# Loading K and Q two rows to a partition, and turning them head by head

## The chip, the cores and the metric

The kernel runs on one core of a Trainium2 chip. A core has TensorE (PE: matmuls, with weight loads shown apart as PEld), VectorE (DVE), ScalarE (ACT), GpSimd (POOL) and SyncE (SP), which here mostly issues transfers, and 16 DMA engines that carry out what SP, ACT and POOL issue. Matmul results lie in PSUM, all other tiles in SBUF. The metric is the time of one execution on the device in microseconds; less is better.

## The reference

Block-sparse attention, followed by a mixture of experts that sends each token to one expert. Cut to what matters:

```python
# q, k, v: (4, 8, 768, 64) float32; blocks of 32 rows, 24 blocks
scores = scale * np.matmul(q, k.transpose(0, 1, 3, 2))
mask = np.abs(blk_i - blk_j) <= 1
mask = mask | (blk_i == 0) | (blk_j == 0) | (blk_i == 23) | (blk_j == 23)
for qb in range(24):
    for kb in sampled_blocks[qb]:          # three random blocks for each
        mask[qb*32:(qb+1)*32, kb*32:(kb+1)*32] = True
attn = softmax(np.where(mask, scores, -1e9))
x = (attn @ v).transpose(0, 2, 1, 3).reshape(3072, 512)
# router: cosine of x with 8 expert vectors, softmax, one expert per token
logits = normalized(x) @ normalized(expert_emb).T / tau
e, gate = argmax(logits), softmax(logits).max()
out[token] = gate * (relu(x[token] @ w1[e]) @ w2[e])   # w1: 8x512x1024
```

## The kernel before, in words

The attention comes first (`attention_fast`), then the experts (`expert_tiles`), whose weights of some 4 MB a tile are loaded by SP while TensorE works on the tile before. A second, exact form of the attention is in the program for data that the fast form cannot take; it has its own loads (`load_pair`) and is not run here. The diff does not touch it.

**Tiles of the attention.** A batch has 768 rows, cut in six chunks of 128 (the chunks are shifted by one block, so that a chunk's first rows meet the first and the last block; chunk 0 is made of rows 736 to 767 and 0 to 95, and `pieces` gives the two row ranges). Two batches are worked on together: pair `s` of 12 stands for one chunk in two batches, and `n` = 2s + i is one chunk of one batch. There are 24 such units, and the main loop runs one in each step; the order is `TURNS` = 0, 2, 1, 3, 4, 5 and so on.

**One step.** For the unit `now`, `score_near` multiplies K with the turned Q (`qt`): neighbouring blocks (L550) and the first and last block (L553); `score_far` does the same with the gathered random blocks `kg` (L575). ScalarE takes exponentials (L558, L560, L580). For the unit of the step before, `weigh_near` and `weigh_far` multiply the exponentials with V (L630), and `normalize` divides and writes `x`. For the unit before that, `turn_x` turns x (L707) and copies it out (L709), and `part_logits` and `sum_logits` make the router's logits (L727, L736). Between the two halves of `weigh_far`, `turn_q` turns the Q of the next unit. Chunk 0 and the last pair of steps have in addition `score_ends` and `weigh_ends`, since the first and the last block see all keys.

**Turning.** Scores need the head dimension on the partitions, so rows of K and Q are turned on TensorE with an identity matrix as the moving operand.
- `load_k` fetches a head pair of one batch: `kraw` has row `p` of chunk `c` on partition `p`, and beside each other the 64 elements of the two heads. `turn_k` turns each chunk's 128 x 128 square (L501: six for a head pair) into two PSUM banks, and one copy (L503) of 128 x 768 brings it to `kt`, on ScalarE for odd head pairs and on VectorE for even ones. After a batch's last pair ScalarE copies the two edge blocks to the end of `kt` (L506).
- `load_q` fetches a pair `s`: a row on each partition, with both batches and eight heads of 64 elements. `turn_q` turns four squares of two heads each (L514) into the one PSUM bank that `turn_x` uses too (`xg_ps`), and two VectorE copies of 64 x 512 (L519) bring them to `qt`, the first head of each couple to partitions 0 to 63 and the second to 64 to 127. The rest of `qt` stays zero, which keeps the heads apart.

**Order.** The attention is written out by hand: each engine works its instructions in the order in which the program gives them (`manual_schedule`). K of the first batches (head pairs 0 to 7) is turned ahead of the loop and in steps 0 and 1; pairs 8 to 15 are turned in steps 10, 11 and 12 (two, three and three pairs), and there the K gathers of `gather_k` (L532, L536, shared between VectorE and GpSimd) come after the turning. The PSUM tiles `ac`, `dps`, `bps` and `kps` take turns on two buffers (`big`).

**Transfers.** SP issues nearly all of them in program order, through `fetch_all`: the V gathers of the pair to come (L478, `vg`, 12 of 128 KB, in one of two buffers, so that they wait until `weigh_far` has freed it), and between each two of these one other load (L476; L480 when no gathers are left): Q, K, or V itself (`vt`). `route` writes x to memory (L834). The first Q loads alone are issued by ScalarE. K has six buffers of a head pair, Q two of a pair.

Of the kernel before, what the change touches and what calls it, by code (L numbers as in the profile page):

```python
# [12 lines left out]
F32 = mybir.dt.float32  # L13
# [7 lines left out]
P = 128  # L21
B, H, S, D = 4, 8, 768, 64
# [3 lines left out]
NC = S // P  # L26
NPAIR = H // 2
# [3 lines left out]
ND, NF = DM // P, F // P  # L31
# [22 lines left out]
DUO = 2  # L54
# [264 lines left out]
def pieces(c, shifted=True):  # L319

    if not shifted:
        return [(slice(0, P), c * P)]
    if c:
        return [(slice(0, P), c * P - BLK)]
    return [(slice(0, BLK), S - BLK), (slice(BLK, P), 0)]
# [61 lines left out]
def pair_chunk(s):  # L387

    a, at = divmod(s, NC)
    return a, at if a == 0 else (at + 1) % NC  # L390
# [8 lines left out]
def of_seq(src, a, i=None):  # L399

    if i is None:
        return src[DUO * a:DUO * (a + 1)].rearrange("i h s d -> s (i h) d")
    return src[DUO * a + i].rearrange("h s d -> s h d")


def in_pair(t, i=None):

    return t.rearrange("p i h e -> p (i h) e") if i is None else t[:, i]


def load_q(k, s, i=None):

    a, c = pair_chunk(s)
    if ("q", s) not in k.raw:
        k.raw["q", s] = k.ld.tile([P, DUO, H, D], F32, name="qraw", tag="qraw", bufs=2)
    t, src = in_pair(k.raw["q", s], i), of_seq(k.q, a, i)
    return [(t[rows], src[lo:lo + rows.stop - rows.start]) for rows, lo in pieces(c)]


def load_k(k, g):  # L420

    b, j = divmod(g, NPAIR)
    k.raw["k", g] = t = k.kld.tile([P, NC, 2, D], F32, name="kraw", tag="kraw", bufs=6)
    return [(t[:, :, h], k.k[b, 2 * j + h].rearrange("(c p) d -> p c d", p=P)) for h in range(2)]


def load_v(k, a, m, i=None):
# [65 lines left out]
def turn_k(k, g):  # L493

    nc = k.nc
    b, j = divmod(g, NPAIR)
    kt = k.kt[b % 2]
    raw = k.raw.pop(("k", g))
    ps = k.big.tile([P, 2, 512], F32, name="kps", tag="big")
    for c in range(NC):  # L500
        nc.tensor.transpose(ps[:, c // 3, c % 3 * P:(c % 3 + 1) * P], raw[:, c].rearrange("p h d -> p (h d)"), k.ident)  # L501
    copy = nc.scalar.copy if g % 2 else nc.vector.tensor_copy
    copy(out=kt[:, j, 0:S].rearrange("p (w t) -> p w t", w=2), in_=ps[:, :, 0:3 * P])  # L503
    if j == NPAIR - 1:
        for i, block in enumerate((NB - 1, 0)):
            nc.scalar.copy(out=kt[:, :, S + i * BLK:S + (i + 1) * BLK], in_=kt[:, :, block * BLK:(block + 1) * BLK])  # L506


def turn_q(k, n):

    raw = in_pair(k.raw["q", n // DUO], n % DUO)
    ps = ring(k, "xg_ps", 0, 1, k.eps, [P, ND, P])
    for j in range(NPAIR):
        k.nc.tensor.transpose(ps[:, j], raw[:, 2 * j:2 * j + 2, :].rearrange("p h d -> p (h d)"), k.ident)  # L514
    k.qt[n] = t = k.qt_ring[k.queries % 2]
    k.queries += 1
    for h in range(2):
        rows = slice(D * h, D * (h + 1))
        k.nc.vector.tensor_copy(out=t[rows, :, h], in_=ps[rows])  # L519


def gather_k(k, n):
# [543 lines left out]
def ring(k, name, i, n, pool, shape):  # L1066

    key = name, i % n
    if key not in k.rings:
        k.rings[key] = pool.tile(shape, F32, name=f"{name}_{i % n}")  # L1070
    return k.rings[key]
# [191 lines left out]
def attention_fast(n, ctx):  # L1263
# [44 lines left out]
    for m in range(2, NC):  # L1308
        fetch_all(n, (), load_v(n, 0, m, 0))
    turn_q(n, 0)  # L1310
    for g in range(NPAIR):
        turn_k(n, g)
        if g + 6 < 2 * NPAIR:
            fetch_all(n, (), load_k(n, g + 6))
# [21 lines left out]
    for s in range(NCH + 1):  # L1336
# [49 lines left out]
        for g in turning.get(s, ()):  # L1386
            turn_k(n, g)
# [282 lines left out]
```

## Time and profile before

| what | value |
|---|---|
| time of the runs shown | 634.98 us median of 3 (632.53 to 637.91) |
| the profiled execution | 636.4 us, its span 634.7 us |
| mean granted TensorE clock | 0.981 |
| TensorE busy, share of the span | 597.9 us, 94% |
| VectorE, ScalarE, GpSimd busy | 235.6, 148.9, 244.8 us |
| end of the attention's last matmul | about 268 us |
| first expert matmul after the weights have landed | 284.9 us |
| packets | 187311, of these 147720 under 512 bytes |
| bytes moved | 170.57 MB, 269 GB/s over the span |
| K loads | 32 of 192 KB, all issued by SP |
| Q loads of a whole chunk | 9 of 512 KB, and parts for the first and last chunks |

The profile's page gives busy time by engine, then the span in 40 equal slices, in which a digit is the busy share in tenths and GB/s what the DMA engines moved. The chain of work that ended last is followed back from the last instruction, at each step to what released it; its rows give the start, the length and the work. A row of the groups has the line, the engine, the operation, what is written from what, the shapes and the count; then the busy time, the mean length of one in ns, and the idle time of the engine just ahead with what ended it. In the rows in order of time the first two numbers are the start and the length, both in us, and several instructions of one kind are merged. In the first 24 us the TensorE clock is below full speed, 0.50 in the second 12 us. A row of TensorE can contain waiting.

### The profile page before, as it was taken

The page shows a single profiled execution, that of the slowest core. Times are in us where ns is not written, and L with a number is a line of the kernel's source. Part 1 is how long each engine was busy: PE and PEld are TensorE (multiplying, and loading weights), DVE is VectorE, ACT ScalarE, POOL GpSimd, SP SyncE. Part 2 cuts the span into 40 slices and gives each one's busy share as a digit, 9 for nine tenths or more (in the row PEclk, how much of TensorE's full clock was granted, in tenths as well). Part 3 has the DMA queues.
Part 4 walks back from the last instruction along what each step waited for, and adds up shares of the span by engine and source line. Part 5 has one row for each costly group of instructions (what it writes and reads, how often), then busy time and mean ns, then how long its engine had stood idle before and what let it go on. Part 6 is the DMA issues. An engine that isn't in the chain of part 4 may idle for free.

```text
span 634.7 us, 18413 instructions
## 1 busy us (share of the span) xinstructions
PE 597.9 (94%) x7542; PEld 456.8 (72%) x7542; DVE 235.6 (37%) x740; ACT 148.9 (23%) x309; POOL 244.8 (39%) x473
## 2 busy tenths in 40 slices
PE   6979997998999999999999999999999999999995
PEld 3868886887778877867777776663777746667773
DVE  2634563666668862337411112112111131112110
ACT  1525554564555544210000000000000000000000
POOL 1716463545656631121134433333344333333432
PEclk7689999999999999999999999999999999999998
DMA  9999999999999992299999999998999998999611
GB/s 171 186 171 196 164 154 179 178 183 171 192 190 176 180 220 77 60 385 396 404 396 406 401 392 362 340 345 317 343 402 406 393 372 315 405 392 407 252 39 34
DMA packets 187311, 170.57 MB, mean 269 GB/s; under 512 B 147720, under 2 KB 147848, under 8 KB 184402
## 3 DMA queue, kind: packets, MB, share of 16 engines
q1 hardware_dynamic: 179906, 155.35, 88.4%
q0 software_dynamic: 5216, 13.43, 5.8%
q8 instruction: 61, 1.00, 0.7%
q10 hardware_dynamic: 2096, 0.52, 0.4%
q14 instruction: 32, 0.26, 0.2%
HBM read 156.65 MB, written 12.90 MB: 267 GB/s over the span
## 4 chain that ended last, share of the span: by engine, by line
PE 75%; DMA 8%; SPq 7%; DVE 4%; ACT 3%; issue 2%; POOL 1%; POOLq 0%; DVEq 0%; ACTq 0%
PE hp L1171 25%; PE yp L1184 24%; PE av L630 7%; SPq L478 5%; DMA vg<-in_v_dram 4%; PE dps L575 3%; PE hp L1216 2%; PE yp L1236 2%; DMA kraw<-in_k_dram 2%; PE ac L550 2%; PE xg_ps L514 2%; DMA w<-in_moe_w_dram 2%; PE ac L553 1%; PE bps L597 1%; PE kps L501 1%
## 5 line engine op out<-in xcount | busy, mean ns | idle before, releaser
L1171 PEld LDWEIGHTS hp<-xgt,w 128*128 128x128 f32 x1472 | 167.8, 192 | 11.3 <-issue 10.2
L1171 PE MATMUL hp<-xgt,w 128*128 128x128 f32 x1472 | 169.2, 275 | 0.8 <-DMA w<-in_moe_w_dram 0.8
L1184 PE MATMUL yp<-w,h 128*128 128x512 f32 x368 | 161.9, 592 | 0.0
L1184 PEld LDWEIGHTS yp<-w,h 128*128 128x128 f32 x368 | 68.1, 190 | 76.5 <-issue 72.2
L1095 POOL DMA_INDIRECT xg<-x_dram,quarter x88 | 89.4, 1016 | 32.3 <-issue 27.7
L1197 POOL DMA_INDIRECT out_dram<-y,slot_l x20 | 20.5, 1026 | 155.8 <-DVE y L1196 155.8
L1174 ACT ACTIVATE h<-hp 128x512 f32<-128x512 f32 x23 | 13.7, 597 | 284.0 <-PE hp L1171 226.9
L1178 DVE TENSOR_SCALAR h<-hp 128x512 f32<-128x512 f32 x23 | 15.9, 692 | 145.6 <-PE hp L1171 145.6
L490 POOL COPY vg<-vt 32x1040 f32<-32x1040 f32 (+1 forms) x45 | 43.0, 956 | 54.8 <-PE av L630 41.7
L532 POOL COPY kg<-kt 128x128 f32 x176 | 43.6, 293 | 35.6 <-ACT kt L503 31.6
L575 PEld LDWEIGHTS dps<-qt,kg 128*64 128x64 f32 x1408 | 47.3, 140 | 2.0 <-issue 1.1
L575 PE MATMUL dps<-qt,kg 128*64 128x64 f32 x1408 | 46.8, 224 | 1.2 <-issue 0.6
L550 PE MATMUL ac<-qt,kt 128*64 128x128 f32 x352 | 45.0, 280 | 2.3 <-DVE qt L519 2.0
L1196 DVE TENSOR_SCALAR y<-yp,gate 128x512 f32<-128x512 f32 x20 | 15.0, 751 | 84.7 <-PE yp L1184 72.6
L553 PE MATMUL ac<-qt,kt 128*64 128x256 f32 (+1 forms) x192 | 44.4, 375 | 0.8 <-ACT kt L506 0.8
L519 DVE COPY qt<-xg_ps 64x512 f32<-64x512 f32 x48 | 33.0, 688 | 30.7 <-PE xg_ps L514 30.3
L550 PEld LDWEIGHTS ac<-qt,kt 128*64 128x64 f32 x352 | 38.5, 139 | 3.8 <-issue 2.2
L580 ACT ACTIVATE pd<-dps,bias 128x256 f32<-128x256 f32 x88 | 34.8, 475 | 17.0 <-PE dps L575 17.0
L630 PE MATMUL av<-vg,pd 128*32 128x65 f32 x1408 | 32.9, 225 | 5.0 <-DMA vg<-in_v_dram 3.0
L630 PE MATMUL av<-st,pac 128*64 128x65 f32 x704 | 31.0, 226 | 3.6 <-DVE x L825 2.3
L630 PEld LDWEIGHTS av<-vg,pd 128*32 128x32 f32 x1408 | 23.8, 110 | 14.3 <-issue 9.2
L630 PEld LDWEIGHTS av<-st,pac 128*64 128x64 f32 x704 | 25.3, 137 | 8.2 <-issue 8.1
(234 smaller groups left out, 614.7 us busy)
## 6 DMA issues: line engine op xcount, KB each, us to landing
w<-in_moe_w_dram SPq DMA_DIRECT2D x52, 2048.0 KB
vg<-in_v_dram SPq DMA_DIRECT2D x132, 128.0 KB
kraw<-in_k_dram SPq DMA_DIRECT2D x32, 192.0 KB
x_dram<-x SPq DMA_DIRECT2D x10, 516.0 KB
qraw<-in_q_dram SPq DMA_DIRECT2D x9, 512.0 KB
w<-in_moe_w_dram SPq DMA_DIRECT2D x8, 512.0 KB
vt<-in_v_dram SPq DMA_DIRECT2D x10, 256.0 KB
vt<-in_v_dram SPq DMA_DIRECT2D x5, 512.0 KB
```

Source lines behind the costliest of these rows:

```text
L478: k.nc.sync.dma_start(out=to, in_=src)
L490: k.nc.gpsimd.tensor_copy(out=k.vg_ring[s % 2][NRAND * BLK:P, g, which(i)], in_=k.vt[m][rows, which(i)])
L519: k.nc.vector.tensor_copy(out=t[rows, :, h], in_=ps[rows])
L532: copy(out=t[:, :, g, s * BLK:(s + 1) * BLK], in_=kt[:, :, bass.ds(shift, BLK)])
L550: nc.tensor.matmul(out[0:D, j, half], lhsT=kt[:, j, at:at + D], rhs=qt[:, j, :, D * half:D * (half + 1)], start=True, stop=True)
L553: nc.tensor.matmul(out[D:P, j, half:2].rearrange("p f h t -> p h f t"), lhsT=kt[:, j, S:S + D], rhs=qt[:, j, :, D * half:P].rearrange("p h ...
L575: nc.tensor.matmul(out[D * r:D * (r + 1), NG * j + g], lhsT=kg[:, j, g, D * r:D * (r + 1)], rhs=qt[:, j, :, cols], start=True, stop=True)
L580: nc.scalar.activation(e[:, :, g].rearrange("p j h t -> p j (h t)"), out.rearrange("p (j g) h t -> p j g (h t)", g=NG)[:, :, g], ACT.Exp, ...
L630: k.nc.tensor.matmul(av[lanes, h // NPAIR, h % NPAIR * P:h % NPAIR * P + D + 1], lhsT=lhsT, rhs=rhs, start=first[0], stop=last, skip_group ...
L1095: k.nc.gpsimd.indirect_dma_start(out=x[:, g], out_offset=None, in_=quarters, in_offset=bass.IndirectOffsetOnAxis(ap=k.quarter[:, g, t:t + ...
L1171: nc.tensor.matmul(hp[:, f, :], lhsT=w1[:, d, (f0 + f) * P:(f0 + f + 1) * P], rhs=xt[:, d, :], start=(d == 0), stop=(d == ND - 1))
L1184: nc.tensor.matmul(yp, lhsT=h[:, f, :], rhs=w2[:, f, :], start=(f == 0), stop=(f == NF - 1))
```

## The change

K and Q are loaded so that a partition holds two neighbouring rows of one head, 512 bytes in one piece, where before a piece was one row of one head, 256 bytes. In the turned square the even rows' head dimension then comes out on partitions 0 to 63 and the odd rows' on 64 to 127. So the copies out of PSUM go by half of the partitions and write every second column of `kt` and `qt`.

- `load_q`: a tile of 128 x 8 x 128. Batch 0 of the pair is on partitions 0 to 63 and batch 1 on 64 to 127, and each batch is its own transfer (two for chunk 0).
- `load_k`: two transfers as before, of half as many pieces.
- `turn_k`: six transposes of 128 x 128 as before, now three for each head; then four copies of 64 x 384, two on VectorE (first head) and two on ScalarE (second head).
- `turn_q`: eight transposes, one a head, of 64 rows with 128 columns; then four VectorE copies of 64 x 256.

```diff
@@ load_q
-        k.raw["q", s] = k.ld.tile([P, DUO, H, D], F32, name="qraw", tag="qraw", bufs=2)
-    t, src = in_pair(k.raw["q", s], i), of_seq(k.q, a, i)
-    return [(t[rows], src[lo:lo + rows.stop - rows.start]) for rows, lo in pieces(c)]
+        k.raw["q", s] = k.ld.tile([P, H, 2 * D], F32, name="qraw", tag="qraw", bufs=2)
+    loads = []
+    for i in range(DUO) if i is None else (i,):
+        for rows, lo in pieces(c):
+            count = rows.stop - rows.start
+            at = D * i + rows.start // 2
+            src = k.q[DUO * a + i, :, lo:lo + count].rearrange("h (p c) d -> p h (c d)", c=2)
+            loads.append((k.raw["q", s][at:at + count // 2], src))
+    return loads
@@ load_k
-    k.raw["k", g] = t = k.kld.tile([P, NC, 2, D], F32, name="kraw", tag="kraw", bufs=6)
-    return [(t[:, :, h], k.k[b, 2 * j + h].rearrange("(c p) d -> p c d", p=P)) for h in range(2)]
+    k.raw["k", g] = t = k.kld.tile([P, 2, NC // 2, 2 * D], F32, name="kraw", tag="kraw", bufs=6)
+    return [(t[:, h], k.k[b, 2 * j + h].rearrange("(w p c) d -> p w (c d)", p=P, c=2)) for h in range(2)]
@@ turn_k
-    for c in range(NC):
-        nc.tensor.transpose(ps[:, c // 3, c % 3 * P:(c % 3 + 1) * P], raw[:, c].rearrange("p h d -> p (h d)"), k.ident)
-    copy = nc.scalar.copy if g % 2 else nc.vector.tensor_copy
-    copy(out=kt[:, j, 0:S].rearrange("p (w t) -> p w t", w=2), in_=ps[:, :, 0:3 * P])
+    for h, copy in enumerate((nc.vector.tensor_copy, nc.scalar.copy)):
+        for w in range(NC // 2):
+            nc.tensor.transpose(ps[:, h, w * P:(w + 1) * P], raw[:, h, w], k.ident)
+        to = kt[D * h:D * (h + 1), j, 0:S].rearrange("r (t c) -> r c t", c=2)
+        for c in range(2):
+            copy(out=to[:, c], in_=ps[D * c:D * (c + 1), h, 0:S // 2])
@@ turn_q
-    raw = in_pair(k.raw["q", n // DUO], n % DUO)
-    ps = ring(k, "xg_ps", 0, 1, k.eps, [P, ND, P])
-    for j in range(NPAIR):
-        k.nc.tensor.transpose(ps[:, j], raw[:, 2 * j:2 * j + 2, :].rearrange("p h d -> p (h d)"), k.ident)
+    raw, rows = k.raw["q", n // DUO], slice(D * (n % DUO), D * (n % DUO + 1))
+    ps = ring(k, "xg_ps", 0, 1, k.eps, [P, ND, P]).rearrange("p j (h t) -> p j h t", h=2)
+    for h in range(H):
+        k.nc.tensor.transpose(ps[:, h // 2, h % 2], raw[rows, h], k.ident[rows, rows])
     k.qt[n] = t = k.qt_ring[k.queries % 2]
     k.queries += 1
     for h in range(2):
-        rows = slice(D * h, D * (h + 1))
-        k.nc.vector.tensor_copy(out=t[rows, :, h], in_=ps[rows])
+        to = t[D * h:D * (h + 1), :, h].rearrange("p j (t c) -> p j c t", c=2)
+        for c in range(2):
+            k.nc.vector.tensor_copy(out=to[:, :, c], in_=ps[D * c:D * (c + 1), :, h])
```

## The prediction

> **What bounds the kernel now.** I read the page's forty slices first, then the chain that ended last, then one step in the order of time, then the groups kept apart by shape. The change touches only the attention part, about the first 268 us; after it the chain is 75% TensorE and holds nothing that the diff touches, so a shift of the attention's end moves the total one for one.
>
> ```profile
> PE   6979997998999999999999999999999999999995
> PEclk7689999999999999999999999999999999999998
> DMA  9999999999999992299999999998999998999611
> GB/s 171 186 171 196 164 154 179 178 183 171 192 190 176 180 220 77 60 385 396 404 396 406 401 392 362 340 345 317 343 402 406 393 372 315 405 392 407 252 39 34
> ```
>
> In slices 1 to 14 (one is 15.9 us) the DMA engines are full, and yet they move only some 178 GB/s (mean of the 14); the same engines move about 400 in the expert part. [...]147720 of the packets are under 512 bytes. TensorE is nearly full too, so both have to be asked. The chain in 94 to 170 us says who wins there:
>
> ```profile
> 95.37 4.06 DMA vg<-in_v_dram
> ...
> 102.74 5.11 DMA x_dram<-x
> ...
> 114.35 5.51 DMA vg<-in_v_dram
> ...
> 130.57 3.02 SPq L478
> ...
> 135.16 5.36 DMA vg<-in_v_dram
> ```
>
> Here the ends are set by transfers and by SP issuing into full queues. To price it I take the steps' starts from the exponentials of `score_near` (L558, L560): steps 0, 1, 2, 4, 10, 13, 18 at 20.8, 28.4, 49.0, 70.4, 125.3, 158.3, 202.3 us. Undisturbed steps (5, 18, 19) take 8.0 us, and there the chain is TensorE. Steps 4 to 10 take 55.0 us for six, so 7.0 over 48; steps 13 to 18 take 43.9 for five, so 3.9 over 40. Steps 10, 11 and 12, with K turned inside, take 33.0. One undisturbed step:
>
> ```profile
> 72.97 0.69 DVE L709 COPY xt<-xg_ps 128x512 f32<-128x512 f32 x1 [2.17 <-PE xg_ps L707]
> ...
> 73.71 0.66 PE L514 MATMUL xg_ps<-ident,qraw 128*128 128x128 f32 x4 [0.19 <-DVE xt L709]
> ...
> 74.41 1.39 DVE L519 COPY qt<-xg_ps 64x512 f32<-64x512 f32 x2 [0.75 <-PE xg_ps L514]
> ...
> 75.72 0.30 PEld L736 LDWEIGHTS yp<-sel,part 128*128 128x128 f32 x2
> 75.73 0.39 PE L736 MATMUL yp<-sel,part 128*128 128x8 f32 x2
> ...
> 76.05 0.32 PE L550 MATMUL ac<-qt,kt 128*64 128x128 f32 x1
> ```
>
> The reader should see a loop: VectorE frees the bank, TensorE turns Q, VectorE copies Q to `qt` until 75.80, and the next step's first score matmul, which needs `qt`, starts at 76.05. The copy is 0.2 us from being the bound.
>
> [...]at L736, whose moving side has 8 columns, the two loads take 0.30 us together and 0.188 each, so the second starts 0.11 after the first.[...]
>
> **The change, part by part.**
>
> ```profile
> L519 DVE COPY qt<-xg_ps 64x512 f32<-64x512 f32 x48 | 33.0, 688 | 30.7 <-PE xg_ps L514 30.3
> L692 DVE TENSOR_TENSOR x<-av,inv 64x256 f32<-64x256 f32 x8 | 3.4, 422 | 0.1
> L503 DVE COPY kt<-kps 128x768 f32<-128x768 f32 x8 | 7.7, 958 | 8.4 <-PE kps L501 8.3
> L503 ACT COPY kt<-kps 128x768 f32<-128x768 f32 x8 | 6.4, 798 | 20.8 <-PE kps L501 20.8
> ```
>
> *Transfers.* K and Q are 12.6 MB, 49152 pieces of 256 bytes, now 24576 of 512. At 178 GB/s over 16 engines a small piece takes 23 ns. The packets above 2 KB average 3.4 KB (132.8 MB over 39.5 thousand) and take 135 ns at 400 GB/s. A line through both gives 32 ns for 512 bytes; bounds are 23 (a price per piece alone, half the time) and 46 (a price per byte alone, no gain). With 32 a head pair of K falls from 2.2 to 1.55 us, a pair's Q from 2.9 to 2.1: 16 x 0.65 + 12 x 0.88 = 21 us of transfer time (0 to 35). Q now comes in halves of 64 partitions, one more issue on SP per pair (two more for an end chunk), some 0.7 us each (median of L476's Q issues, waiting for room included), ahead of V gathers in SP's order: about 9 us of issue, in a queue that gets 21 us relief. I count it at nothing beside the relief; without it, half of it could show.
>
> What the relief is worth is what waits for it:
> - Prologue. K pairs land earlier, which brings step 0 some 2 us forward; its turning and copying give 1 us back by step 1 (the Q turning at the cold clock, 0.8, and the copies). In step 1 TensorE waits from 33.0 to 36.8 for two K pairs, 2.9 us beyond their turning: gone, with eight pairs x 0.65 plus Q saved by then. Sum -3.5, a little of it needed for two more turnings there.
> - Steps 4 to 10: -7.0 at most. K for the second half and V press hardest here; a pair of steps still asks for gathers, V, Q and x of about 17 us in its 16 to 17. I take -6.
> - Steps 13 to 18: -3.9 at most; I take -3.6.
>
> *Turning Q.* Four transposes of 128x128 (0.11 us apart) become eight with 64 rows, 128 weight columns and 64 moving. If weight loads set the pace (0.093 to 0.11) that is 0.75 to 0.88 in place of 0.44; if only moving columns did, 0.44. I take +0.36 (0 to 0.44). Two copies of 64x512 (0.689) become four of 64x256; the row of that size is 0.422, so 1.69 for 1.38: +0.31, with 0.2 us of slack. TensorE's own work after the turning, 1.74 us, moves along, so a step grows by 0.36 + 0.31 - 0.2 = 0.45 us (0 to 0.55). Behind the copies stand the denominators, x and the K gathers of VectorE; x has 2.7 us until its bank is wanted. This hits 18 steps outside 10 to 12: +8.1. Where the trace has VectorE itself on the chain (200 to 214) up to 0.7 is possible.
>
> *Turning K.* TensorE's count stays. Each pair was one copy of 128x768 on VectorE (0.958) or ScalarE (0.798), in turn; now VectorE and ScalarE each do two of 64x384. From 512 and 768 elements VectorE runs 1.05 ns an element, ScalarE (0.597 at 512) 0.79, so 0.554 and 0.497: 1.11 and 0.99 per pair on each. In step 11 VectorE is the bound:
>
> ```profile
> 140.08 0.96 DVE L503 COPY kt<-kps 128x768 f32<-128x768 f32 x1 [1.04 <-PE kps L501]
> 140.95 0.92 DVE L532 COPY kg<-kt 128x128 f32 x4
> 141.79 1.03 DVE L536 COPY kg<-kt 128x128 f32<-128x128 f32 x4
> 142.75 1.38 DVE L519 COPY qt<-xg_ps 64x512 f32<-64x512 f32 x2
> ```
>
> The K copies stand ahead of the gathers and these ahead of `qt`, which the next scores await. After: ScalarE has 2.1 us of V stacking ahead (137.84 to 139.97), then pairs 10 and 11, then the edge copy: gathers from 142.5, `qt` at 146.1 for 144.13, +1.9. By the same walk step 10 (two pairs, four VectorE copies for one long one, 0.2 of slack used) +1.6, step 12 +0.9. Together +4.4, whatever the transfers do.
>
> *Sum.* -3.5 - 6 - 3.6 + 4.4 + 8.1 = -0.6 us on an execution of 636.4 us (span 634.7, 1.7 around it). The median of the runs shown is 634.98, 1.4 below that execution; carried over, **634.5 us**.
>
> **The rivals.**
> - *The turning is cheap* (0.22). Transposes at the pace of 64 moving columns leave 0.11 us a step: 2 in place of 8.1, giving 628.4; with a smaller copy price or all stalls gone, down to 625. For it: in `score_far` matmuls of 64 columns run 29 ns apart (64 in 1.86 us). Against: those load 64 weight columns, and L736 shows 0.11 for 128. I take 627.
> - *The pieces bring nothing* (0.15). If 512 bytes cost 46 ns, the stalls of 94 to 200 stay and hide part of the new work: 0.45 on ten TensorE-bound steps, 4.4 for K, 1.5 in the prologue and some 1 us of extra issues on SP: +12, 647. Against: with its larger pieces the expert part moves twice as much in the same time.
> - *Writes to every second column are slow* (0.15). The place is the `qt` copy, between Q's turning and the next scores, in all 18 steps. A halved write rate adds 256 x 1.05 = 0.27 us to each of four copies, 19 us in all, and some 5 in steps 10 to 12: about 658. It decides from 0.4 us a step on (18 x 0.4 = 7 us). For it: no row writes so.[...]
> - That transfers aren't cut to 512 bytes is excluded by both sides being contiguous over it.
>
> **How the numbers follow.** The forecast has 0.48 and its own range 628.7 to 641 (gain of the stalls +-3, step price +-0.2 on 18 steps). About 1%, 6.3 us, is what a measurement of this kernel tells from no change. Faster by more: the cheap turning, 0.22. Within: 0.48. Slower: 0.15 + 0.15 = 0.30. The range reaches to the cheap case's end and to the case without gain, 625 to 647; slow writes, 0.15, lie beyond.
>
> **What would show it.** Packets under 512 bytes down by 49 thousand; SP's issues and V landings off the chain in 94 to 200 us. L514's successor with 192 transposes, about 0.1 us apart; 96 copies of `qt` at 0.42; 32 of `kt` on VectorE at 0.55 and 32 on ScalarE at 0.50. Undisturbed steps of 8.45 us; steps 10 to 12 taking 37. The prediction is wrong if undisturbed steps stay at 8.0 (then faster), if V gathers still end the chain, or if the strided copies last over 0.55 us.

## The result and the profile after

The changed kernel takes 663.73 us (median; 661.25 to 664.13) beside 634.34 us for the kernel before on the same chip: a ratio of 1.043 [1.0379, 1.0482], with a 95% interval in the brackets. It is slower, outside the range that was given. The profiled execution took 664.13 us, its span 662.4. In what follows a ratio is always to runs of the kernel before on the same chip, and microseconds derived from a ratio are the ratio less 1 times 635. A stretch of a profile comes from one execution, and the four executions of the kernel before lie 5 us apart: a difference of two or three microseconds in one stretch is a hint, no more.

The forty slices of the page of the changed kernel (one is 16.6 us):

```profile
PE   5589999887789989999999999999999999999995
PEclk7689999977788998999999999999999999999999
DMA  9998699999399997229999999999899998999711
GB/s 175 211 171 169 118 165 188 188 183 160 56 151 178 165 136 182 76 79 383 399 401 401 403 391 400 334 333 331 319 404 391 408 374 310 405 397 398 285 49 33
```

Where before slices 1 to 14 were full on the DMA row, there is now a hole in slice 11 (166 to 182 us, 56 GB/s), and the granted clock is at 0.7 to 0.8 in slices 9 to 13. The transfers no longer bound this stretch; TensorE is the slow one, and part of its slowness is its clock. Packets under 512 bytes fell from 147720 to 98744, and those from 512 bytes to 2 KB rose from 128 to 24704, by 24576: as many as the change has pieces of 512 bytes. By the start of the steps, read as in the prediction, and with the prediction's own terms put on the same stretches:

| stretch | before, us | after, us | difference | forecast |
|---|---|---|---|---|
| start to step 4 | 70.4 | 78.2 | +7.8 | -2.6 |
| steps 4 to 10 | 55.0 | 51.5 | -3.5 | -3.3 |
| steps 10 to 13, K turned inside | 33.0 | 50.2 | +17.2 | +4.4 |
| steps 13 to 18 | 43.9 | 47.4 | +3.5 | -1.3 |
| steps 18 to 23 | 40.1 | 43.2 | +3.1 | +2.3 |
| step 23 to the end | 392.3 | 391.8 | -0.5 | 0 |

The two stretches in which K is turned (the prologue with steps 0 and 1, and steps 10 to 12) hold nearly all of the loss. The view of waits says what TensorE stood for there (the engine, what it was about to do, what it waited for; total us, times, longest). The row of the groups below it has the same line before:

```profile
PEld kps L508 <- DVE kt L511: 26.9, 16, 2.6
PE kps L508 <- DVE kt L511: 22.4, 16, 2.3
...
ACT kt L511 <- PE kps L508: 27.8, 15, 5.1
```

```profile
L501 PE MATMUL kps<-ident,kraw 128*128 128x128 f32 x96 | 17.0, 332 | 7.1 <-DMA kraw<-in_k_dram 6.0 <-ACT kt L503 0.9 <-DVE kt L503 0.2
```

Sixteen times, once for each head pair, TensorE waits for VectorE's copies of K (PE and PEld are two records of one wait). Before, the line waited for K to land (6.0 us) and hardly for copies (0.9 and 0.2). In the order of time in step 11, where three pairs are turned one after another, first after, then before:

```profile
148.54 0.49 PE L508 MATMUL kps<-ident,kraw 128*128 128x128 f32 x3
149.35 1.11 DVE L511 COPY kt<-kps 64x384 f32<-64x384 f32 x2
150.52 0.88 PE L508 MATMUL kps<-ident,kraw 128*128 128x128 f32 x6 [1.49 <-DVE kt L511]
151.29 0.99 ACT L511 COPY kt<-kps 64x384 f32<-64x384 f32 x2
151.43 1.12 DVE L511 COPY kt<-kps 64x384 f32<-64x384 f32 x2 [0.97 <-PE kps L508]
152.61 0.87 PE L508 MATMUL kps<-ident,kraw 128*128 128x128 f32 x6 [1.22 <-DVE kt L511]
...
154.77 0.90 PE L508 MATMUL kps<-ident,kraw 128*128 128x128 f32 x3 [1.29 <-DVE kt L511]
155.60 1.10 PE L639 MATMUL av<-vg,pd 128*32 128x65 f32 x32
```

```profile
137.23 1.66 PE L501 MATMUL kps<-ident,kraw 128*128 128x128 f32 x12
...
139.10 0.87 PE L501 MATMUL kps<-ident,kraw 128*128 128x128 f32 x6 [0.20 <-DVE kt L503]
```

After: three transposes of the first head, VectorE's two copies of it, and only then the three of the second head (recorded in one row with the next pair's first three). The wait is 1.2 to 1.5 us at each second head. Before, the six of a pair followed each other without a stop, and the wait ahead of the third pair was 0.20 us. The row at 155.60 shows the second cost: 32 matmuls of `av` take 1.10 us where an undisturbed step has 0.66; TensorE's clock has dropped (granted 0.50 from 154.7 to 160). The table of windows has it for steps 10 to 12 (columns: stretch, length, busy us and count of PE, PEld, DVE, ACT, POOL, then the clock, DMA share, GB/s), first after, then before:

```profile
129.80:180.00 50.20, 38.64 (x672) 32.94 (x670) 26.42 (x81) 22.31 (x51) 16.07 (x39) 0.80 0.79 134
```

```profile
125.30:158.30 33.00, 29.85 (x662) 26.20 (x660) 20.38 (x62) 17.54 (x39) 15.26 (x36) 1.00 1.24 177
```

Of the 17.2 us, 8.8 are TensorE busy for longer with nearly the same work (672 records for 662) at a clock of 0.80, and 8.4 are TensorE idle (11.6 in place of 3.2). The groups of the changed kernel show that the copies themselves are as forecast:

```profile
L528 DVE COPY qt<-xg_ps 64x256 f32<-64x256 f32 x96 | 40.6, 423 | 31.4 <-PE xg_ps L522 30.4
L508 PE MATMUL kps<-ident,kraw 128*128 128x128 f32 x96 | 19.4, 341 | 22.5 <-DVE kt L511 22.4
...
L511 DVE COPY kt<-kps 64x384 f32<-64x384 f32 x32 | 17.7, 554 | 18.7 <-PE kps L508 18.4
L511 ACT COPY kt<-kps 64x384 f32<-64x384 f32 x32 | 15.9, 496 | 28.0 <-PE kps L508 27.8
```

The mean lengths are 423, 554 and 496 ns; the prediction had 422, 554 and 497. So writing every second column makes these copies no longer than was forecast, and the rival of slow writes, which asked for 0.27 us more on each copy of `qt`, is out. The stretch 94 to 112 us of the chain that ended last shows what became of the transfers' part:

```profile
97.37 0.70 DVE xt L718
98.12 0.71 PE xg_ps L522 x8
...
102.94 1.86 PE dps L584 x64
105.90 0.70 DVE xt L718
106.64 0.72 PE xg_ps L522 x8
```

Where `vg` and SP's issues ended the chain before, it is now the loop of the step, 8.5 us long here and 8.28 where nothing disturbs it.

### The profile page after: what moved, and what is told of

It is laid out like the page before. It is cut to its first block, busy times and chain, and to the rows that moved or that the text cites. A ratio compares the mean times of both kernels' runs of the same rounds, so it can differ in the third digit from the quotient of the medians.

```text
span 662.4 us, 18737 instructions
## 1 busy us (share of the span) xinstructions
PE 612.2 (92%) x7638; PEld 470.4 (71%) x7638; DVE 251.1 (38%) x812; ACT 158.5 (24%) x333; POOL 245.0 (37%) x473
## 2 busy tenths in 40 slices
DMA packets 162913, 170.59 MB, mean 258 GB/s; under 512 B 98744, under 2 KB 123448, under 8 KB 160002
## 4 chain that ended last, share of the span: by engine, by line
PE 82%; DVE 9%; DMA 3%; issue 3%; ACT 2%; POOL 0%; ACTq 0%; SPq 0%; POOLq 0%; DVEq 0%
PE hp L1180 24%; PE yp L1193 23%; PE av L639 7%; PE dps L584 6%; PE ac L559 4%; DVE qt L528 3%; PE ac L562 3%; PE xg_ps L522 3%; PE kps L508 2%; DVE kt L511 2%; PE hp L1225 2%; PE yp L1245 2%; DVE xt L718 2%; PE xg_ps L716 2%; DMA w<-in_moe_w_dram 2%
## 5 line engine op out<-in xcount | busy, mean ns | idle before, releaser
L1180 PEld LDWEIGHTS hp<-xgt,w 128*128 128x128 f32 x1472 | 167.8, 192 | 11.6 <-issue 10.2
L528 DVE COPY qt<-xg_ps 64x256 f32<-64x256 f32 x96 | 40.6, 423 | 31.4 <-PE xg_ps L522 30.4
L559 PE MATMUL ac<-qt,kt 128*64 128x128 f32 x352 | 48.7, 295 | 1.7 <-DVE qt L528 1.4
L562 PE MATMUL ac<-qt,kt 128*64 128x256 f32 (+1 forms) x192 | 48.4, 400 | 1.0 <-ACT kt L514 1.0
L559 PEld LDWEIGHTS ac<-qt,kt 128*64 128x64 f32 x352 | 42.4, 150 | 3.2 <-PE yp L745 2.1
L508 PE MATMUL kps<-ident,kraw 128*128 128x128 f32 x96 | 19.4, 341 | 22.5 <-DVE kt L511 22.4
L589 ACT ACTIVATE pd<-dps,bias 128x256 f32<-128x256 f32 x88 | 34.7, 475 | 17.2 <-PE dps L584 17.0
L639 PE MATMUL av<-st,pac 128*64 128x65 f32 x704 | 33.4, 236 | 3.5 <-issue 2.4
L639 PEld LDWEIGHTS av<-st,pac 128*64 128x64 f32 x704 | 27.3, 147 | 9.0 <-issue 8.9
```

The costliest lines, as they stand in the source:

```text
L508: nc.tensor.transpose(ps[:, h, w * P:(w + 1) * P], raw[:, h, w], k.ident)
L528: k.nc.vector.tensor_copy(out=to[:, :, c], in_=ps[D * c:D * (c + 1), :, h])
L559: nc.tensor.matmul(out[0:D, j, half], lhsT=kt[:, j, at:at + D], rhs=qt[:, j, :, D * half:D * (half + 1)], start=True, stop=True)
L562: nc.tensor.matmul(out[D:P, j, half:2].rearrange("p f h t -> p h f t"), lhsT=kt[:, j, S:S + D], rhs=qt[:, j, :, D * half:P].rearrange("p h ...
L589: nc.scalar.activation(e[:, :, g].rearrange("p j h t -> p j (h t)"), out.rearrange("p (j g) h t -> p j g (h t)", g=NG)[:, :, g], ACT.Exp, ...
L639: k.nc.tensor.matmul(av[lanes, h // NPAIR, h % NPAIR * P:h % NPAIR * P + D + 1], lhsT=lhsT, rhs=rhs, start=first[0], stop=last, skip_group ...
```

## The experiments

Each edit is to the kernel named; expectations are as put down before the run.

**Turn both heads of a pair, then copy** (in the changed kernel). It takes away what the second head's transposes wait for; transposes and copies stay the same.

```diff
-    for h, copy in enumerate((nc.vector.tensor_copy, nc.scalar.copy)):
+    for h in range(2):
         for w in range(NC // 2):
             nc.tensor.transpose(ps[:, h, w * P:(w + 1) * P], raw[:, h, w], k.ident)
+    for h, copy in enumerate((nc.vector.tensor_copy, nc.scalar.copy)):
         to = kt[D * h:D * (h + 1), j, 0:S].rearrange("r (t c) -> r c t", c=2)
```

> The changed kernel with one thing moved: turn_k turns both heads of a pair first (six transposes) and then makes its four copies. Theory W (the order of turn_k made a wait: the second head's transposes stand until VectorE has copied the first head, 16 times, 49 us of TensorE idle under that name): steps 10 to 13 fall from 50.2 us to about 37, step 1 starts near 28 us in place of 37.4, the time is 641 us (636 to 646). Rival C (the copies themselves, more of them and to every second column, are what costs): the wait moves to the next user of the buffers and the time stays at 656 or more.

Measured: 647.75 us, 1.0174 [1.0117, 1.0231]. The order costs 16 us of the loss. 11 us are left. That is less than was expected: step 1 starts at 31.4 us, not near 28, and steps 10 to 12 still take 47.3 us, not 37. So the wait between the heads is the largest single part of the loss, but not all of it, and in steps 10 to 12 the smaller part.

**The K part alone, the Q part alone, and the K part with both heads turned first.** The first two take the diff's K or Q functions into the kernel before; the third adds the edit above.

> Only the K part of the change (load_k and turn_k as changed, load_q and turn_q as before). Theory W: most of the loss is here, 656 us (652 to 660), the step without turning back at 8.0 us for 8.3, steps 10 to 13 still at 48 to 50 us. Rival Q (Q's eight short transposes and four copies in each of 24 steps make the loss): 640 us or less.

> Only the Q part of the change (load_q and turn_q as changed, load_k and turn_k as before). Theory W: 636 us (632 to 641): 0.3 us on each undisturbed step, part of it hidden by stalls that stay, some of the transfers relieved. Rival Q: 650 us or more.

> Only the K part, with both heads of a pair turned first and copied then. Theory W: no wait and no Q cost, so 633 us (628 to 638), with steps 10 to 13 at 35 to 37 us and fewer stalls in steps 4 to 10. Rival C: 650 us or more.

Measured: K alone 650.16, 1.0222 [1.0154, 1.0289]; Q alone 644.6, 1.012 [1.0058, 1.0182]; K alone with both heads first 637.93, 1.0034 [1.0009, 1.0059]. So K costs 14 us, of which the order makes 12; Q costs 7.6, where its expectation had 1 or so. Both together would be 22 and the change lost 27, but the intervals of the three ratios leave some 7 us open, so a rest that belongs to neither alone is not shown. The K part turned first still has no gain from its transfers, and its steps 10 to 12 take 42.9 us for the expected 35 to 37. Two rows of its waits, and the last pair of step 11 in the order of time, show why:

```profile
ACT kt L506 <- DVE kt L506: 12.6, 11, 3.8
...
PE kps L502 <- ACT kt L506: 4.8, 3, 2.1
```

```profile
138.93 0.88 PE L502 MATMUL kps<-ident,kraw 128*128 128x128 f32 x6 [2.12 <-ACT kt L506]
139.92 1.12 DVE L506 COPY kt<-kps 64x384 f32<-64x384 f32 x2 [1.62 <-PE kps L502]
...
141.15 1.03 ACT L506 COPY kt<-kps 64x384 f32<-64x384 f32 x2 [0.71 <-DVE kt L506]
```

Both heads are turned by 139.8, but ScalarE begins only at 141.15, when VectorE is through with its two copies of the other head (139.92 and 1.12): they take turns on the tile. TensorE has to wait until the last of the four is done before it gets a buffer again (2.12 us at 138.93).

**The wait alone, and two copying engines alone** (in the kernel before, with its loads and its Q). First three chunks, VectorE's copy of 128 x 384, three chunks, ScalarE's copy; then all six chunks and the same two copies.

```diff
-    for c in range(NC):
-        nc.tensor.transpose(ps[:, c // 3, c % 3 * P:(c % 3 + 1) * P], raw[:, c].rearrange("p h d -> p (h d)"), k.ident)
-    copy = nc.scalar.copy if g % 2 else nc.vector.tensor_copy
-    copy(out=kt[:, j, 0:S].rearrange("p (w t) -> p w t", w=2), in_=ps[:, :, 0:3 * P])
+    for w, copy in enumerate((nc.vector.tensor_copy, nc.scalar.copy)):
+        for c in range(3 * w, 3 * w + 3):
+            nc.tensor.transpose(ps[:, w, c % 3 * P:(c % 3 + 1) * P], raw[:, c].rearrange("p h d -> p (h d)"), k.ident)
+        copy(out=kt[:, j, w * S // 2:(w + 1) * S // 2], in_=ps[:, w, 0:3 * P])
```

> The kernel before, its loads, its Q and its column order kept, with the order of the changed turn_k alone: three chunks turned, VectorE copies them (128x384), three more turned, ScalarE copies them. Theory W (the wait that this order makes is what costs, without small steps in the columns and without larger pieces): 645 us (640 to 650), TensorE idle under VectorE's kt copies 16 times, a lower granted clock in steps 10 to 12. Rival C (the number and stride of the copies): 637 us or less.

> As the run before it (loads and Q of the kernel before), but all six chunks turned first, then one half copied by VectorE and one by ScalarE. Theory W: the wait is gone, 634 us (630 to 638); if ScalarE's copy starts only when VectorE's has ended, the two engines cannot share one PSUM tile here, and each pair takes the sum of both copies (about 1.05 us). If they run side by side, 632 or less.

Measured: 638.3, 1.0043 [1.0019, 1.0067], and 638.63, 1.0034 [1.0015, 1.0053]. The expectation of 645 fell: the same sixteen waits are there (TensorE idle under VectorE's copies for 13.2 and 17.8 us, by its two records), but they cost 2.7 us. A wait is one copy of 0.56 us long here and two in the change (1.11), and the clock in steps 10 to 12 stays at 1.00. The order of the loop is cheap with half the copying and dear with all of it. In the second run ScalarE stands 13 times until VectorE's copy is done (18.8 us): the two engines take turns there too.

**All four copies of a pair on one engine** (K part alone, both heads turned first; the engine alternates from pair to pair).

> Only the K part, both heads turned first, all four copies of a pair on one engine (VectorE for even pairs, ScalarE for odd ones). Theory S (two engines on one PSUM tile take turns, so the split buys nothing; on one engine each, two pairs run side by side): steps 10 to 13 fall from 42.9 us to 36 to 40, 632 us (627 to 637). Rival C (the amount of copying is what costs): 637 us or more, as with the split.

Measured: 639.3, 1.0061 [1.004, 1.0082]; steps 10 to 12 take 45.4 us, and the expected gain did not come. A pair's tile is held here for four copies of half the partitions, about 2.1 us, where it was one of 0.96 or 0.80. That this is what costs is likely, but was not tried by itself.

**A PSUM tile for each head**, in the whole change and in the K part alone, with the order of the change.

```diff
-    ps = k.big.tile([P, 2, 512], F32, name="kps", tag="big")
     for h, copy in enumerate((nc.vector.tensor_copy, nc.scalar.copy)):
+        ps = k.big.tile([P, 2, 512], F32, name="kps", tag="big")
```

> The whole change, with one edit: each head of a pair is turned into a PSUM tile of its own (two of the two buffers of big) in place of one tile with a bank for each head. Order of transposes and copies as in the change. Theory D (the second head's transposes, and ScalarE's copies behind VectorE's, wait for the tile, not for a bank or an engine): TensorE's idle time under VectorE's K copies falls from 49 us to 15 or less, the copies of the two engines overlap, 640 to 648. Rival B (two copies of 64x384 on each engine, four for a pair, are themselves what TensorE waits for): the waits move to the next pair's buffer and the time stays at 655 or more.

> The K part of the change alone, with a PSUM tile of its own for each head. Theory D: about what turning both heads first gave or better, 631 to 638. Rival B: 645 or more, near the K part alone (650).

Measured: 649.1, 1.0212 [1.0146, 1.0278], and 638.62, 1.0022 [0.9999, 1.0046]. The whole change with a tile for each head regains 13.8 us, a little less than expected, and this settles the wait. The second head was in another bank all along; only the tile that it belongs to has changed, and TensorE's idle time under VectorE's copies of K falls from 49.3 us, both records together, to 0.8. What remains is 6.5 us (by PE's record) under ScalarE's copies of the pair before, and the two engines now work side by side:

```profile
PE kps L508 <- ACT kt L511: 6.5, 7, 1.2
...
PE kps L508 <- DVE kt L511: 0.8, 1, 0.8
```

```profile
142.90 0.52 PE L508 MATMUL kps<-ident,kraw 128*128 128x128 f32 x3 [0.75 <-DVE kt L511]
143.46 1.12 DVE L511 COPY kt<-kps 64x384 f32<-64x384 f32 x2 [0.71 <-PE kps L508]
143.56 0.99 ACT L511 COPY kt<-kps 64x384 f32<-64x384 f32 x2
144.60 0.87 PE L508 MATMUL kps<-ident,kraw 128*128 128x128 f32 x6 [1.18 <-ACT kt L511]
```

ScalarE's two copies at 143.56 take 0.99 us beside VectorE's two of 1.12, as long as in the changed kernel (0.99, and 1.11 to 1.12). In the change it was the program's waits, set for the whole tile, that kept them apart. The clock in steps 10 to 12 is 1.00 in this run. But side by side brings the K part no further than both heads first did (1.0022 for 1.0034), and in both runs with a tile for each head steps 10 to 12 take 41.3 us, 8.3 more than before.

**K's transfers alone, on 128 and on 64 partitions** (in the kernel before, which turns and copies as ever; K's order is left undone in both).

```diff
-    k.raw["k", g] = t = k.kld.tile([P, NC, 2, D], F32, name="kraw", tag="kraw", bufs=6)
-    return [(t[:, :, h], k.k[b, 2 * j + h].rearrange("(c p) d -> p c d", p=P)) for h in range(2)]
+    k.raw["k", g] = t = k.kld.tile([P, NC, 2 * D], F32, name="kraw", tag="kraw", bufs=6)
+    return [(t[D * h:D * (h + 1)], k.k[b, 2 * j + h].rearrange("(w p c) d -> p w (c d)", p=D, c=2)) for h in range(2)]
```

(This is the form on 64 partitions; the one on 128 has the change's `load_k`.)

> The kernel before with K's transfers in pieces of 512 bytes and nothing else: turning and copies as before, so that K's rows and heads come out in another order than the reference's (that part of the result is left undone). Theory T (pieces of 512 bytes relieve the transfers): 627 us (622 to 631), from the prologue and the stalls of steps 4 to 10 and 13 to 18. Rival N (the larger pieces bring nothing): 634 us or more.

> As the run with K's transfers alone (512-byte pieces, two transfers for a head pair, turned as before), but each head's 384 pieces land on 64 partitions, six on each, in place of 128 partitions with three. The order of K's rows is left undone. Theory H (a transfer to 64 partitions loses what the larger pieces save): 635 to 641, where 128 partitions gave 630.6. Rival I (only the number of issues counts, which is the same here): 629 to 632.

Measured: 630.64, 0.9923 [0.9888, 0.9957] on 128 partitions; 635.21, 0.9971 [0.9948, 0.9993] on 64. So K's larger pieces are worth 4.9 us, and with each transfer on half of the partitions 1.8. The difference of 3 us is just clear of its interval (0.4 to 5.7). Both have the same packets on the main queue, 167618 for 179906 before.

What one piece costs a DMA engine does not come out of these runs. The pages give the time of the queue's packets as a share of 16 engines' span: 8977 us before, 8905 and 8972 here. But the run with the wait alone has 8883 with the transfers of the kernel before, and the share passes 1 in the windows above (1.24), so the times of packets overlap.

**Q's turning alone and Q's transfers alone** (in the kernel before).

```diff
@@ turning alone
-        k.nc.tensor.transpose(ps[:, j], raw[:, 2 * j:2 * j + 2, :].rearrange("p h d -> p (h d)"), k.ident)
+        for c in range(2):
+            k.nc.tensor.transpose(ps[:, j, D * c:D * (c + 1)], raw[rows, 2 * j:2 * j + 2, :].rearrange("p h d -> p (h d)"), k.ident[rows, rows])
-        k.nc.vector.tensor_copy(out=t[rows, :, h], in_=ps[rows])
+        for c in range(2):
+            part = slice(D * c, D * (c + 1))
+            k.nc.vector.tensor_copy(out=t[rows, :, h, part], in_=ps[rows, :, part])
@@ transfers alone (load_q as in the change)
+            k.nc.tensor.transpose(ps[:, j], raw[:, NPAIR * (n % DUO) + j], k.ident)
```

> The kernel before with its own loads; only the turning of Q has the size of the change: eight transposes of 64 rows with 128 columns, and four VectorE copies of 64x256 (to a contiguous half of the columns). It turns one half of a chunk's rows twice and leaves the other half out. Theory T (the turning is Q's whole cost): 24 units by the 0.28 us that an undisturbed step grew in the changed kernel, some of it in the prologue at half clock: 5 to 9 us over before, so 641 to 645, and nothing left for the transfers. Rival L (half of Q's net cost of 9.3 us comes from loads on 64 partitions and the added issues): 637 to 640, with undisturbed steps of 8.2 us.

> The kernel before with the change's transfers of Q alone (512-byte pieces, each batch on 64 partitions); Q is turned by four transposes of 128x128 and two copies of 64x512 as before (eight transposes for the four units of the first two pairs), so the order of Q's rows is left undone. Theory T (the loads neither help nor hurt): 634 to 637. Rival L (a transfer to 64 partitions[...] and the added issues hold V gathers up): 638 to 641. Third case (they help as K's did): 629 to 632; then Q's net cost of 9.3 us is more than 12 us of turning.

Measured: turning 637.98, 1.0025 [1.0005, 1.0044]; transfers 641.27, 1.0081 [1.0049, 1.0114]. That is 1.6 and 5.1 us of Q's 7.6. Rival L held in both: the transfers that were to bring relief are the larger cost. The turning in the order of time, in the changed kernel and then in this run:

```profile
81.56 0.71 PE L522 MATMUL xg_ps<-ident,qraw 64*128 64x64 f32 x8 [0.19 <-DVE xt L718]
82.31 1.73 DVE L528 COPY qt<-xg_ps 64x256 f32<-64x256 f32 x4 [0.81 <-PE xg_ps L522]
...
84.19 0.29 PE L559 MATMUL ac<-qt,kt 128*64 128x128 f32 x1 [0.17 <-DVE qt L528]
```

```profile
172.04 0.57 PEld L515 LDWEIGHTS xg_ps<-ident,qraw 64*128 64x128 f32 x8 [0.36 <-DVE xt L712]
172.05 0.71 PE L515 MATMUL xg_ps<-ident,qraw 64*128 64x64 f32 x8 [0.19 <-DVE xt L712]
172.79 1.53 DVE L522 COPY qt<-xg_ps 64x256 f32<-64x256 f32 x4 [0.80 <-PE xg_ps L515]
174.43 0.32 PE L553 MATMUL ac<-qt,kt 128*64 128x128 f32 x1
```

Eight transposes take 0.71 us where four took 0.66, so the forecast's +0.36 is +0.05. The four copies take 1.73 in the change (before: 1.39), and in this run 1.53 with contiguous writes: each copy is as long (0.42), but they follow at 0.37 us on average instead of 0.44. Shown one by one, the copies of this run start at 172.79, 173.13, 173.56 and 173.90: 0.34 us after one that read the same half of the partitions, 0.43 after one that read the other half, with contiguous writes all along. In the change every copy reads the other half than the one before it, and all follow at 0.43 to 0.44 (82.31, 82.75, 83.19, 83.62). So the change of half goes with the later start; every second column on the same half was not run. An undisturbed step is 8.28 us in the change and 8.05 here.

**What costs in Q's transfers.** Extra issues alone (each batch its own transfer, 256-byte pieces on 128 partitions); larger pieces alone on 128 partitions, twice, since the first of these runs gave the experts one tile of tokens more.

```diff
@@ more issues
-    t, src = in_pair(k.raw["q", s], i), of_seq(k.q, a, i)
-    return [(t[rows], src[lo:lo + rows.stop - rows.start]) for rows, lo in pieces(c)]
+    loads = []
+    for n in range(DUO) if i is None else (i,):
+        t, src = in_pair(k.raw["q", s], n), of_seq(k.q, a, n)
+        loads += [(t[rows], src[lo:lo + rows.stop - rows.start]) for rows, lo in pieces(c)]
+    return loads
@@ larger pieces, second form
+    if s >= 2 and c:
+        lo = max(0, c * P - BLK - P)
+        src = k.q[DUO * a + 1, :, lo:lo + 2 * P].rearrange("h (p c) d -> p h (c d)", c=2)
+        return [(k.raw["q", s].rearrange("p i (h c) d -> p (i h) (c d)", c=2), src)]
```

> The kernel before with 256-byte pieces of Q on 128 partitions; only each batch of a pair comes by a transfer of its own, as in the change (25 Q issues on SP in place of 14). Theory I (eleven more issues of 0.6 to 0.7 us, in a queue that is full up to 220 us, are what Q's loads cost): 640 to 642. Rival H (it is the 64 partitions): 634 to 637.

> As the run with Q's transfers alone (Q in 512-byte pieces, turned as before), but each whole chunk pair comes in one transfer of 512 KB that fills 128 partitions, as many issues as in the kernel before. For that it fetches 256 neighbouring rows of one batch in place of 128 rows of two, so the values of Q are other rows; the number and size of pieces are those of the change. Theory H (64 partitions in a transfer, or the added issues, are what cost; the pieces themselves help): 630 to 633, like K's loads. Rival N (Q's larger pieces bring nothing wherever they land): 634 to 637. Rival P (larger pieces of Q hurt): 640 or more.

> The kernel before, with Q's pieces alone: the nine whole chunk pairs after the first two come in one transfer each, as before, but in 512-byte pieces on 128 partitions; all other Q loads, the turning and the number of issues are those of the kernel before. It fetches 256 neighbouring rows of one batch in place of 128 rows of two, so these units compute with other rows of Q; the batch and the rows are chosen so that the experts get as many tiles of tokens as before (in the run with one transfer a pair they got one tile more). Theory H (the pieces themselves help; 64 partitions, first loads and added issues are what cost): 631 to 634. Rival N (Q's larger pieces bring nothing in this place): 635 to 637.

Measured: issues 637.71, 1.0036 [1.0015, 1.0057]. First run with larger pieces 674.09, 1.0626, which says nothing on transfers: the experts' second product (`yp`) runs 384 times in it and 368 in all others. By the reference's formula, its rows of Q send 193 tokens to an expert that has 192 otherwise, six full groups of 32. Its attention's step 23 begins at 240.9 us, before: 242.4. Second run 634.08, 0.9962 [0.9941, 0.9983]. So Q's pieces by themselves bring 2.4 us, eleven more issues cost 2.3 (less than the issues' own forecast and more than the rival's), and some 5 us (2 to 8 with the intervals of the three runs) are left for what only the change's loads have: 64 partitions to a transfer, and the first Q loads of the prologue. There step 0 starts at 22.3 to 22.9 us in the three runs that have the change's first loads and the old K, for 20.8 before; with K on 64 partitions and the old first loads of Q it is 22.6.

**A version with the gain and without the cost.** K in the change's pieces, but turned by twelve matmuls of 64 columns, so that the two heads of a row parity come out on 128 partitions and one copy does; then the same for head pairs 0 to 7 alone.

```diff
-    for c in range(NC):
-        nc.tensor.transpose(ps[:, c // 3, c % 3 * P:(c % 3 + 1) * P], raw[:, c].rearrange("p h d -> p (h d)"), k.ident)
+    for c in range(2):
+        for w in range(NC // 2):
+            for h in range(2):
+                nc.tensor.matmul(ps[D * h:D * (h + 1), c, w * P:(w + 1) * P], lhsT=raw[:, h, w, c * D:(c + 1) * D], rhs=k.ident, start=True, stop=True)
     copy = nc.scalar.copy if g % 2 else nc.vector.tensor_copy
-    copy(out=kt[:, j, 0:S].rearrange("p (w t) -> p w t", w=2), in_=ps[:, :, 0:3 * P])
+    copy(out=kt[:, j, 0:S].rearrange("r (t c) -> r c t", c=2), in_=ps[:, :, 0:3 * P])
```

> The kernel before with K alone in pieces of 512 bytes, Q as before, and K put in order by another turning: twelve matmuls with the identity, each of 64 columns (one head, even or odd rows), so that both heads of a row parity come out on 128 partitions; then one copy of 128x768 for a head pair as before, on VectorE and ScalarE in turn, which writes every second column. Theory W (the copies in four parts and the order of turning cost, not the pieces nor the strided writes): 630 to 632, as with K's loads alone; twelve matmuls of 64 columns take what six of 128 took, since in the kernel before matmuls with 64 weight columns run 29 ns apart. Rival M (a weight load and a matmul of 64 columns cost nearly what 128 do): 0.6 us on each of 16 pairs, about half of it on the path, so 635 to 640.

> K in 512-byte pieces with turning by twelve matmuls of 64 columns and one copy for a head pair, as in the run by parity, but only for head pairs 0 to 7 (prologue and steps 0 and 1); pairs 8 to 15, turned in steps 10 to 12, are loaded and turned as in the kernel before. In the run by parity steps 10 to 12 took 39.0 us for 33.0, and the rest came out ahead. Theory W: that loss goes and the earlier start stays, 630 to 633. Rival M (without the smaller transfers of pairs 8 to 15 the stalls of steps 4 to 10 come back and eat it): 634 to 636.

Measured: 634.66, 0.9972 [0.9948, 0.9996]; and 636.97, 1.002 [0.9991, 1.0049]. The first is faster than the change and 0.3% faster than the kernel before, which is no gain in practice. Its trace records 24 matmuls of 64 columns for a pair, not 12 (384 in all), 0.058 us apart, so that turning a pair takes 1.4 us for 0.7: the expectation had counted one record for a matmul. Steps 10 to 12 take 39.0 us. Sparing the second half did not help: that version is not told from the kernel before. Its steps 10 to 12 take 33.2 us, but steps 4 to 10 take 55.6, as before; one trace does not show that the second half's pieces make that difference.

## Why the prediction was wrong

- **The step that failed first is "TensorE's count stays"**, with what it took along: "now VectorE and ScalarE each do two of 64x384 ... 1.11 and 0.99 per pair on each". Durations and counts were right. What was put at nothing is what stands between the two heads: three transposes, a copy by one engine, three transposes into the same tile. The diff has this loop in plain sight, and the kernel before has no such place. It costs 12 us in the K part (2.2% against 0.3%) and 16 in the whole change, by wait and by the clock that drops after it; with a tile for each head 13.8 us of it come back. By its own sign, "steps 10 to 12 taking 37" against 50.2, the step is refuted.
- **K's turning itself was also priced too low.** The forecast had +4.4 us for steps 10 to 12, from four shorter copies in place of a long one. Without any wait between the heads, the K part takes 8.3 to 9.9 us more there than before (41.3 with a tile for each head, 42.9 with both heads first). In the whole time these two versions lie 6.3 and 7.0 us above K's transfers alone, each within some 2.7. Whether the engines take turns or work side by side makes no difference that the runs can tell; what the versions share is four copies of half the partitions for each pair. That these are the cause was not tried by itself.
- **"The turning of Q, +8.1"** had the right place and the wrong size. Undisturbed steps grew by 0.28 us, not 0.45, which over 18 steps makes 5 us (an estimate); the turning alone, with contiguous writes, cost 1.6. The eight transposes were priced at 0.09 to 0.11 us each, the spacing of loads of 128 rows and 128 columns before the change (0.09 on average at 73.71 to 73.99 us, 0.11 at L736); that 64 rows would cost as much was the author's estimate. Here the loads of 64 rows and 128 columns follow at about 0.063 us (eight starts from 81.56 to 82.00), so the measurement decides for the lower bound of 0: +0.05 for +0.36. The copies' +0.31 was +0.34.
- **"I count it at nothing beside the relief"** on Q's halves of 64 partitions and their issues is the third failed step. Issues cost 2.3 us, and on 64 partitions K's pieces kept 1.8 us of their 4.9. The prediction gave the 64 partitions no price of their own.
- **The relief by larger pieces** was counted as 21 us of transfer time worth 13.1 us of the whole (3.5, 6 and 3.6). Alone and on 128 partitions, K's pieces brought 4.9 us and Q's 2.4; the 32 ns for a piece of 512 bytes were not measured. That the size of the pieces makes the difference between 178 and 400 GB/s was the author's estimate; with K's larger pieces alone, slices 1 to 14 moved 182 GB/s for 178 (means). The 51.5 us of steps 4 to 10, for 51.7 forecast, look like a hit but are not shown to be one: the two runs with only K's copying changed keep the pieces of 256 bytes and take 51.4 and 51.3 there. Both enter the stretch 2 to 3 us later than the kernel before, the change 8 us later. The match may be luck.
- **Prologue, -3.5**: K's loads alone do bring step 1 forward by 2.7 us (25.6 for 28.4). In the change it starts 9 us late (37.4). The K part alone has it at 37.2 and the Q part alone at 29.5, so nearly all of this is K's turning.
- **Steps 13 to 18, -3.6**: undisturbed steps are 8.28 us there too, but step 14 takes 12.9, with 1.4 us in which TensorE waited for nothing that the profile shows and a low clock after it (0.52 from 195 to 202 us). Such stretches lie in most runs at other places. Their cause stays open.
- **The rivals**: the total lies beyond all of them. "The turning is cheap" had the transposes right and the total wrong. "Pieces bring nothing" had the right sign for a wrong reason. "Slow writes" came nearest with 658, by luck: nothing in the length of the copies of `qt` speaks for it (0.423 us each); its weight of 0.15 was the author's estimate, since no row of before writes so. The wait between heads was not among them.
- One reading was off without harm: the 75% of TensorE is its share of the chain over the whole span. After 268 us it is about 93%, and nothing of the diff is there, as was said.

## What to carry to other kernels

When a loop is split so that producer and consumer of one PSUM tile alternate inside it, read the new order as a chain: in a program whose waits are set by tile, as here, a write after a copy waits for that copy even in another bank, as long as the tile is one (49.3 us of such waits with one tile, 0.8 with one for each head). Give each part its own tile or finish all writes before the first copy; both were tried here and gave back 14 and 16 us. Count, too, how many copies stand between a write and the buffer's next use, not only how long each engine is busy. A transfer that is made larger in its pieces but lands on half of the partitions may keep little of the gain (K's kept 1.8 us of 4.9): measure the load alone before rewriting what consumes it. And when one stretch comes out as forecast, look whether it does so in a run without the change as well.

## What the runs showed of the hardware

- Three waits of 1.2 to 1.5 us within 6 us went together with half clock on TensorE for the next few us (32 matmuls of `av` in 1.10 us for 0.66), and so did a single one of 1.4 us in step 14 of the changed kernel (granted 0.52 on average from 195 to 202 us). The waits of the run with the order alone, 0.8 us on average, left the clock of steps 10 to 12 at 1.00. What brings the clock down was not tried by itself.
- K in pieces of 512 bytes made the kernel 4.9 us faster when a transfer fills 128 partitions, 1.8 when it fills 64.
- On VectorE, copies with every second column written, at a step of 8 bytes, were as long as contiguous ones: 0.423 against 0.417 us for 64 x 256, 0.961 against 0.958 for 128 x 768. On ScalarE they were longer: 0.870 against 0.798 for 128 x 768.
- VectorE's copies out of PSUM of 64 x 256 started 0.34 us after one that read the same half of the partitions, 0.43 to 0.44 after one that read the other.
- Transposes of 64 rows and 128 columns, with 64 moving columns, loaded their weights 0.063 us apart; those of 128 rows, with 128 moving columns, 0.11 us apart after the first two (73.71, 73.77, 73.88 and 73.99 us in the kernel before). Rows and moving columns were not changed one at a time.
